# Order of the first two head pairs written out by hand, mask constants copied by ACT instead of DMA, bias loaded later, more output buffers

## Chip, cores, metric

The kernel runs on one core of a Trainium2 chip. The metric is device time in microseconds (us) of one execution. A ratio in this text is the mean time of one kernel's fast runs over the mean time of the other's fast runs of the same rounds; it is therefore not quite the ratio of the medians that are quoted. A profile is one execution, and its times count from the start of its span.

PE is TensorE's matmul part, PEld its weight loads, DVE is VectorE, ACT is ScalarE, POOL is GpSimd, and SP is SyncE, which only issues DMAs here. In the profile lines `qs` is q with its selection, `trm` and `tr` are transposes, `kTp` is k transposed, `kmm` and `km` are the extremes of k, `rq` the two signed parts of q, `ub` the bounds, `sc` scores, `e` exps, `acc` attention values, `mlp` a result of the MLP and `o` the output. An eviction is ACT's copy of a finished matmul result into a buffer.

## What the kernel computes

Four batches, eight heads, 768 positions, head size 64. Attention looks only at the six best chunks of 32 keys for each query; a gated MLP follows.

```python
k_min, k_max = min and max of k over each chunk of 32 keys
ub    = sum_d max(q*k_min, q*k_max)               # upper bound of a score for each query and chunk
ub    = where(causal by chunk, ub, -1e9)
mask  = (chunk of key is among the 6 largest ub) & (key <= query)
attn  = softmax(where(mask, q@k.T / sqrt(64), -1e9))
x     = (attn @ v) of all heads side by side       # (4, 768, 512)

h     = relu(x @ w_in);  u, v = halves of h
v_n   = (v - mean(v)) / sqrt(var(v) + 1e-6)
out   = (u * (w_spatial @ v_n + b_spatial[:, None])) @ w_out
```

## The kernel before: what the change touches

The work is cut into 16 pairs of heads, four per batch. Each pair has a preparation (k transpose, chunk extremes, q transpose, bounds, top six, selection, transposes and copies of the selection and q into an operand `a`) and then two times six groups of scores, each followed by an exp on ACT. One half of each key operand `kh` holds a mask constant, `expand`, which each buffer of the ring must be given once.

The program is written as a list of steps at "beats", and a scheduler sets the final order of instructions on each engine. Only for PE, and only for beats below zero, the written order is kept.

```python
NB = 4
kh_ring = [[ring.tile([P, S], F16, ...) for hi in range(2)] for i in range(NB)]

def init_kh(i):                       # the mask constant of ring place i
    for hi, (d0, d1) in enumerate(HALF):
        if i < 2:
            nc.scalar.copy(kh_ring[i][hi][d0:d1, :], expand)
        else:
            nc.sync.dma_start(out=kh_ring[i][hi][d0:d1, :], in_=expand)
# ... cut ...
def a_copy(self, hi):
    if self.i >= 8: return
    copy = nc.vector.tensor_copy if self.i == 0 and hi == 0 else nc.scalar.copy
    copy(self.a[:, :, hi, :], self.tr.rearrange("d (t s) -> d t s", s=P))
# ... cut: the output of one tile of 128 rows, six for each batch ...
o_sb = ml.tile([P, DM], F32, tag="o", name="o", bufs=3)
nc.scalar.copy(o_sb, o_ps)
nc.sync.dma_start(out=out[b, ti * P:(ti + 1) * P, :], in_=o_sb)
# ... cut: order of the start ...
at(B0, init_masks)                    # B0 = -30
at(B0, load_k, 0, 0, 1); at(B0, load_k, 0, 1, 1)
for i in range(NB):
    at(B0 if i < 2 else -8, init_kh, i)
for i, p in enumerate(pairs):
    t0 = i * BEATS                    # BEATS = 12
    if i == 1: t0 += 4
    if i == 0: ...                    # pair 0: one step after the other at B0 + 1
        continue
    at(t0 - 27, p.k_transpose); at(t0 - 22, p.k_max); at(t0 - 21, p.q_transpose)
    # ... cut ...
```

The softmax here doesn't subtract the row's maximum and nothing guards it: scores larger than these inputs give would overflow.

## Time and profile before

| | before |
|---|---|
| median of the runs | 211.34 us (211.15 to 211.51) |
| span of the profiled execution | 209.2 us |
| first exp (pair 0) | 16.70 us |
| pair 1's first exp | 25.46 us |
| first MLP eviction | 58.41 us |

The chain of waits of the kernel before, as shares of the span by engine:

```profile
PE 65%; ACT 17%; DVE 5%; POOL 5%; DMA 4%; issue 3%; POOLq 0%; ACTq 0%
```

The shares alone say "PE-bound". The table by stretches says where. Its columns are the stretch in us, its length, the busy time of PE, PEld, DVE, ACT and POOL with the number of instructions, the granted clock, and the DMA share and GB/s. (The DMA share is the time of all packets added up over the time of 16 engines; it can exceed 1.) Kernel before:

```profile
25.46:58.41 32.95, 29.08 (x446) 22.08 (x445) 28.81 (x92) 30.94 (x68) 26.86 (x35) 1.00 1.98 171
61.00:105.00 44.00, 43.32 (x499) 27.84 (x497) 40.38 (x118) 37.00 (x80) 17.68 (x18) 1.00 1.73 130
105.00:150.00 45.00, 44.53 (x450) 26.46 (x449) 38.54 (x123) 37.06 (x81) 8.34 (x9) 1.00 0.81 142
150.00:185.00 35.00, 34.77 (x268) 18.20 (x267) 18.05 (x39) 23.28 (x49) 4.33 (x5) 1.00 0.44 102
```

From 61 to 185 us PE hardly idles, so time won earlier should be kept there. From 25 to 58 us ACT is fullest, with PE and DVE close behind. Before that single waits set the time: from 9 to 16 us PE is busy 4.16 us of 7, DVE 2.73 and ACT 3.07. Only POOL, which issues the loads of q, k and v one after the other, is busy throughout. These are ACT's (start, duration, what; in brackets the idle time before it and what ended it), kernel before:

```profile
10.85 0.70 ACT L215 ACTIVATE rq<-trm 128x640 f16<-128x640 f16 x1 [0.93 <-DVE rq L213]
11.45 0.78 ACT L197 COPY kh_1_89<-kTp 64x768 f16<-64x768 f16 x1
14.99 0.80 ACT L260 COPY a<-trm 128x768 f16<-128x768 f16 x1 [2.76 <-PE trm L254]
16.70 1.57 ACT L274 ACTIVATE e<-sc 128x512 f16<-128x512 f32 x3 [0.90 <-PE sc L272]
...
18.80 2.78 ACT L274 ACTIVATE e<-sc 128x512 f16<-128x512 f32 x6
22.23 1.25 ACT L274 ACTIVATE e<-sc 128x512 f16<-128x512 f32 x3 [0.65 <-PE sc L269]
```

And these are the three places where PE stood for a DMA in the start, timeline of the kernel before:

```profile
9.60 0.69 PE L208 MATMUL trm<-identity,qs_83 128*128 128x128 f16 x5 [2.91 <-DMA qs_83<-in_q_dram]
...
18.66 0.50 PE L173 MATMUL kTp<-identity,k 128*128 128x128 f16 x6 [0.39 <-DMA k<-in_k_dram]
...
21.64 0.44 PE L208 MATMUL trm<-identity,qs_84 128*128 128x128 f16 x5 [0.65 <-DMA qs_84<-in_q_dram]
```

The first is pair 0's q. The other two are pair 2's k and q, whose transposes stand in PE's order among pair 0's scores, so that those scores wait for pair 2's landing.

The end, ACT's timeline of the kernel before, shows the third to the sixth of the last six output copies:

```profile
202.25 0.59 ACT L440 COPY o<-mlp 128x512 f32<-128x512 f32 x1 [0.28 <-PE mlp L391]
204.32 1.79 ACT L440 COPY o<-mlp 128x512 f32<-128x512 f32 x3 [1.48 <-DMA out_dram<-o]
```

The fourth copy waits 1.48 us until an earlier output DMA has freed one of three buffers.

### The profile page before, as it was taken

The numbers are of one execution on the slowest core, as the hardware profiler recorded it, in microseconds if no ns is written. First come the engines' busy times: TensorE is split into PE (matmuls) and PEld (weight loads), VectorE is DVE, ScalarE is ACT, GpSimd is POOL, SyncE is SP. The second block draws the span as 40 slices with busy tenths as digits, with TensorE's granted clock in tenths as the row PEclk, the third lists the DMA queues.
The fourth block names the chain that finished last, engine by engine and source line by source line (L and its number), as shares of the span: only waits on it lengthen the run. The fifth ranks groups of instructions, "written<-read, shape, count | busy, mean of one in ns | idle before, by whom it ended". The sixth has DMA issues, their size and how long they took to land.

```text
span 209.2 us, 5074 instructions
## 1 busy us (share of the span) xinstructions
PE 187.0 (89%) x1922; PEld 114.8 (55%) x1922; DVE 154.1 (74%) x453; ACT 155.7 (74%) x323; POOL 79.6 (38%) x99
## 2 busy tenths in 40 slices
PE   0359799798999999999999999999999999999991
PEld 0256577575666665656664656556555554444440
DVE  6348989888889989899888799888547356366520
ACT  4638798999997899785979996668999821666033
POOL 7995697595991364237114111111111110000000
PEclk9999999999999999999999999999999999999998
DMA  6999999999999699979998932948792115530365
GB/s 38 158 128 155 141 172 155 181 177 173 172 163 165 50 117 125 152 128 123 155 258 183 175 55 50 128 86 148 192 172 66 38 28 100 179 147 3 75 157 219
DMA packets 115496, 27.66 MB, mean 132 GB/s; under 512 B 110352, under 2 KB 111888, under 8 KB 115472
## 3 DMA queue, kind: packets, MB, share of 16 engines
q0 software_dynamic: 76512, 12.19, 88.2%
q1 hardware_dynamic: 38960, 15.15, 36.0%
q8 instruction: 15, 0.25, 0.5%
q14 instruction: 9, 0.07, 0.1%
HBM read 24.38 MB, written 6.29 MB: 147 GB/s over the span
## 4 chain that ended last, share of the span: by engine, by line
PE 65%; ACT 17%; DVE 5%; POOL 5%; DMA 4%; issue 3%; POOLq 0%; ACTq 0%
PE mlp L391 38%; PE sc L269 11%; ACT e L274 9%; PE acc L292 8%; ACT a L260 3%; DMA k<-in_k_dram 3%; PE ub L225 2%; POOL qs_83 L341 2%; PE kTp L173 2%; PE tr L208 1%; DVE vn L415 1%; POOL k L332 1%; ACT o L440 1%; DMA out_dram<-o 1%; ACT u L423 1%
## 5 line engine op out<-in xcount | busy, mean ns | idle before, releaser
L274 ACT ACTIVATE e<-sc 128x512 f16<-128x512 f32 x192 | 97.2, 552 | 15.6 <-PE sc L269 13.7
L391 PE MATMUL mlp<-w_in_sb,xT 128*128 128x512 f16 x192 | 52.9, 379 | 0.0
L281 POOL TENSOR_SCALAR_AFFINE_SELECT e<-e 128x768 f16<-128x768 f16 x24 | 20.8, 867 | 68.7 <-ACT e L274 68.6
L292 PEld LDWEIGHTS <-e 128*128 128x128 f16 x672 | 31.6, 97 | 17.5 <-DVE x_2178 L300 1.0
L391 PE MATMUL mlp<-vn,wsT 128*128 128x512 f16 x144 | 37.3, 379 | 0.0
L440 ACT COPY o<-mlp 128x512 f32<-128x512 f32 x24 | 14.1, 590 | 20.8 <-PE mlp L391 18.6
L403 DVE BATCH_NORM_STATS2 stats<-vraw 128x6 f32<-128x512 f32 x24 | 16.6, 693 | 13.5 <-ACT vraw L401 13.1
L391 PE MATMUL mlp<-w_out_sb,gT 128*128 128x512 f16 x96 | 25.1, 379 | 0.0
L391 PEld LDWEIGHTS <-xT 128*128 128x128 f16 x192 | 17.2, 97 | 12.4 <-issue 0.4
L430 DVE SCALAR_TENSOR_TENSOR g<-mlp,b_col,u 128x512 f16<-128x512 f32 x24 | 17.9, 747 | 7.3 <-PE mlp L391 6.2
L391 PEld LDWEIGHTS <-wsT 128*128 128x128 f16 x144 | 12.9, 98 | 10.4
L181 DVE TENSOR_REDUCE kmm<-kTp 128x24 f16<-128x768 f16 x16 | 15.1, 945 | 3.4 <-PE kTp L173 3.2
L401 ACT ACTIVATE vraw<-mlp 128x512 f32<-128x512 f32 x24 | 14.4, 601 | 3.0 <-PE mlp L391 3.0
L423 ACT ACTIVATE u<-mlp 128x512 f16<-128x512 f32 x24 | 14.3, 597 | 1.7 <-PE mlp L391 1.5
L330 POOL DMA_DIRECT2D k<-in_k_dram x14 | 14.4, 1042 | 2.5 <-PE kTp L173 1.8
L185 DVE TENSOR_REDUCE kmm<-kTp 128x24 f16<-128x768 f16 x16 | 15.1, 943 | 0.0
L173 PE MATMUL kTp<-identity,k 128*128 128x128 f16 x96 | 8.6, 230 | 6.3 <-POOL tri L144 5.9
L391 PEld LDWEIGHTS <-gT 128*128 128x128 f16 x96 | 9.1, 98 | 8.9
L292 PE MATMUL acc<-vt_80,e 128*128 128x65 f16 x252 | 13.7, 193 | 0.0
L415 DVE TENSOR_SCALAR vn<-vraw,mv,rstd 128x512 f16<-128x512 f32 x24 | 11.8, 544 | 2.2 <-ACT rstd L413 2.1
L292 PE MATMUL acc<-vt_81,e 128*128 128x65 f16 x252 | 13.0, 193 | 0.2 <-DVE x_3135 L300 0.2
L299 DVE RECIPROCAL rec<-acc 128x6 f32<-128x6 f32 x32 | 6.0, 187 | 6.5 <-PE acc L292 6.2
(165 smaller groups left out, 337.5 us busy)
## 6 DMA issues: line engine op xcount, KB each, us to landing
out_dram<-o SPq DMA_DIRECT2D x24, 256.0 KB, 2.3
k<-in_k_dram POOLq DMA_DIRECT2D x14, 192.0 KB, 8.2
vt_80<-in_v_dram POOLq DMA_DIRECT2D x3, 384.0 KB, 8.7
qs_84<-in_q_dram POOLq DMA_DIRECT2D x6, 192.0 KB, 7.5
vt_81<-in_v_dram POOLq DMA_DIRECT2D x3, 384.0 KB, 8.8
ws_raw<-in_moe_w_spatial_dram POOLq DMA_DIRECT2D x6, 192.0 KB, 7.6
w_in_sb<-in_moe_w_in_dram POOLq DMA_DIRECT2D x8, 128.0 KB, 6.6
qs_85<-in_q_dram POOLq DMA_DIRECT2D x4, 192.0 KB, 7.2
```

The lines of the kernel that those rows point to most:

```text
L181: nc.vector.tensor_reduce(self.kmm[:, 0, :], self.kT.rearrange("d (c ch) -> d c ch", ch=CHUNK), axis=AX.X, op=Alu.max)
L185: nc.vector.tensor_reduce(self.kmm[:, 1, :], self.kT.rearrange("d (c ch) -> d c ch", ch=CHUNK), axis=AX.X, op=Alu.min, negate=True)
L269: mm(sc[:, col:col + n], lhsT=self.kh[hi][:, t * P:(t + 1) * P], rhs=self.a[:, q0 // P:(q0 + n) // P, hi, :], start=True, stop=not diag)
L274: nc.scalar.activation(out=self.e[hi][:, g * 512:g * 512 + width], in_=sc[:, 0:width], func=Act.Exp, scale=scale)
L281: nc.gpsimd.affine_select(out=blk, in_=blk, compare_op=Alu.is_ge, fill=0.0, base=0, channel_multiplier=-1, pattern=[[0, NQT], [1, P]])
L292: mm(self.av[:, qi, :], lhsT=self.e[hi][:, c:c + P], rhs=self.v[hi][:, t, 0:D + 1], start=first and n == 0, stop=last and n == len(blocks) ...
L330: nc.gpsimd.dma_start(out=t[:, :, :, 1 - hi, :].rearrange("p x t d -> p (x t) d"), in_=source(k, b, h, 2))
L391: mm(st[group][:, 0:cols], lhsT=lhsT, rhs=rhs, start=(j == 0), stop=(j == n - 1))
L403: nc.vector.bn_stats(stats, st["vraw"][:, ti, :])
L423: nc.scalar.activation(st["u"][:, ti, :], h, func=Act.Relu)
L430: nc.vector.scalar_tensor_tensor(g, in0=vs, scalar=b_col[:, ti:ti + 1], in1=st["u"][:, ti, :], op0=Alu.add, op1=Alu.mult)
L440: nc.scalar.copy(o_sb, o_ps)
```

## The change

The intent is a shorter start. (1) The mask constants of ring places 2 and 3 are copied by ACT instead of by four SP DMAs. (2) The preparation of pairs 0 and 1 is one list in a hand-written order, PE's written order is kept up to beat 5, pair 1's first copy of `a` goes to DVE, and pairs 2 and 3 are prepared later. (3) The second half of the first k load, which is pair 1's k, is issued before the masks are made, and the spatial bias is loaded later, by POOL. (4) The output tile has six buffers. The diff is shortened; left out are `init_ring(2)`, `init_kh(0)` and `init_kh(1)`, which are now listed at the start by name, and two conditions rewritten without effect.

```diff
     def init_kh(i):
         for hi, (d0, d1) in enumerate(HALF):
-            if i < 2:
-                nc.scalar.copy(kh_ring[i][hi][d0:d1, :], expand)
-            else:
-                nc.sync.dma_start(out=kh_ring[i][hi][d0:d1, :], in_=expand)
+            nc.scalar.copy(kh_ring[i][hi][d0:d1, :], expand)
@@
-            copy = nc.vector.tensor_copy if self.i == 0 and hi == 0 else nc.scalar.copy
+            copy = nc.vector.tensor_copy if self.i < 2 and hi == 0 else nc.scalar.copy
@@
-        nc.sync.dma_start(out=b_col, in_=moe_b_spatial...)
+        nc.gpsimd.dma_start(out=b_col, in_=moe_b_spatial...)
@@
-                o_sb = ml.tile([P, DM], F32, tag="o", name="o", bufs=3)
+                o_sb = ml.tile([P, DM], F32, tag="o", name="o", bufs=6)
@@
-    at(B0, init_masks)
     at(B0, load_k, 0, 0, 1)
     at(B0, load_k, 0, 1, 1)
+    at(B0, init_masks)
@@
-        if i == 1:
-            t0 += 4
-        if i == 0:
-            ...                                  (the list of pair 0, cut)
+        if i < 2:
             continue
-        at(t0 - 27, p.k_transpose)
+        t0 += 4 if i < 4 else 0
+        at(t0 - (22 if i < 4 else 27), p.k_transpose)
@@
+    p, n = pairs[0:2]
+    for beat, *step in (
+            ... (B0 + 1, p.top, 1), (B0 + 1, p.select), (B0 + 1, init_kh, 2), (B0 + 1, init_kh, 3),
+            (B0 + 1, p.a_transpose, 0), (B0 + 1, p.a_copy, 0), (B0 + 1, n.k_transpose),
+            (B0 + 1, p.a_transpose, 1), (B0 + 1, n.k_max), (B0 + 1, p.a_copy, 1), (B0 + 1, n.k_min),
+            (B0 + 1, n.k_operand, 0), (0, n.q_transpose), (1, n.q_parts, 0), (1, n.k_bounds), (1, n.q_parts, 1),
+            (1, n.k_operand, 1), (2, n.bounds), (3, n.top, 0), (3, n.top, 1), (4, n.select), ...):
+        at(beat, *step)
@@
-        for beat in sorted(b for b in beats if b < 0):
+        for beat in sorted(b for b in beats if b < 6):
```

More of the change, by code (lines that the diff above doesn't have):

```diff
@@ L195, in k_operand @@
             d0, d1 = HALF[1 - hi]
-            copy = nc.scalar.copy if self.i == 0 else nc.vector.tensor_copy
+            copy = nc.scalar.copy if self.i < 1 else nc.vector.tensor_copy
             copy(self.kh[hi][d0:d1], self.kT[d0:d1])
@@ L213, in q_parts @@
                 nc.vector.tensor_scalar(self.rq[:, 0, P:S], in0=self.tr[:, P:S], scalar1=0.0, scalar2=None, op0=Alu.max)
-            elif self.i == 0:
+            elif self.i < 1:
                 nc.scalar.activation(self.rq[:, 1, P:S], self.tr[:, P:S], func=Act.Relu, scale=-1.0)
@@ L374, in load_b @@
     def load_b():
-        nc.sync.dma_start(out=b_col, in_=moe_b_spatial.rearrange("(to ti) -> ti to", ti=P))
+        nc.gpsimd.dma_start(out=b_col, in_=moe_b_spatial.rearrange("(to ti) -> ti to", ti=P))
     def mlp(b):
@@ L471 @@
     at(B0, init_ring, 1)
-    at(-6, init_ring, 2)
-    for i in range(NB):
-        at(B0 if i < 2 else -8, init_kh, i)
+    at(B0, init_ring, 2)
+    at(B0, init_kh, 0)
+    at(B0, init_kh, 1)
     at(40, load_b)
@@ L494 @@
         t0 = i * BEATS
-        if i == 1:
-            t0 += 4
-        if i == 0:
-            for step in ((p.k_transpose,), (p.k_max,), (p.k_min,), (p.k_operand, 0), (p.q_transpose,),
-                         (p.q_parts, 0), (p.k_bounds,), (p.q_parts, 1), (p.k_operand, 1), (p.bounds,), (p.top, 0), (p.top, 1), (p.select,),
-                         (p.a_transpose, 0), (p.a_copy, 0), (p.a_transpose, 1), (p.a_copy, 1)):
-                at(B0 + 1, *step)
+        if i < 2:
             continue
-        at(t0 - 27, p.k_transpose)
+        t0 += 4 if i < 4 else 0
+        at(t0 - (22 if i < 4 else 27), p.k_transpose)
         at(t0 - 22, p.k_max)
@@ L519 @@
         at(t0 - 6, p.a_copy, 1)
+    p, n = pairs[0:2]
+    for beat, *step in (
+            (B0 + 1, p.k_transpose), (B0 + 1, p.k_max), (B0 + 1, p.k_min), (B0 + 1, p.k_operand, 0),
+            (B0 + 1, p.q_transpose), (B0 + 1, p.q_parts, 0), (B0 + 1, p.k_bounds),
+            (B0 + 1, p.q_parts, 1), (B0 + 1, p.k_operand, 1), (B0 + 1, p.bounds), (B0 + 1, p.top, 0),
+            (B0 + 1, p.top, 1), (B0 + 1, p.select), (B0 + 1, init_kh, 2), (B0 + 1, init_kh, 3), (B0 + 1, p.a_transpose, 0), (B0 + 1, p.a_copy, 0),
+            (B0 + 1, n.k_transpose), (B0 + 1, p.a_transpose, 1), (B0 + 1, n.k_max), (B0 + 1, p.a_copy, 1), (B0 + 1, n.k_min),
+            (B0 + 1, n.k_operand, 0),
+            (0, n.q_transpose), (1, n.q_parts, 0), (1, n.k_bounds), (1, n.q_parts, 1),
+            (1, n.k_operand, 1), (2, n.bounds), (3, n.top, 0), (3, n.top, 1), (4, n.select), (5, n.a_transpose, 0),
+            (5, n.a_copy, 0), (6, n.a_transpose, 1), (6, n.a_copy, 1)):
+        at(beat, *step)
     for j in range(NDO):
```

## The prediction

> **What bounds the kernel now.** The chain of waits gives PE 65% and ACT 17% of the span. The table by stretches shows three stages. From 61 to 185 us PE is busy over 98%, so what reaches 61 us earlier should end earlier. From 25.46 to 58.41 us ACT is busy 30.94 of 32.95 us, PE 29.08. Before that is a start of single dependent steps: the timeline has the first exp at 16.70 us and pair 1's first at 25.46. The end (185 to 209) is paced by PE, then by output.
>
> **The start.** The timeline has pair 0's q transposes at 9.60 us, 2.9 us idle for q's landing; those loads took 3.9 and 4.9 us from issue, the first k loads 3.2 and 3.5. Between lie four SP copies of mask constants, at 5 to 9 us. The DMA records show q/k packets falling from about 700 per us to 425 to 570 while those run. The Trainium skill ("DMA: Bandwidth & Descriptors", Issuing engines are not separate DMA queues) says that DMAs of all issuers share 16 DMA engines; this trace agrees. Without the copies I estimate that q lands 1.2 us earlier. ACT's kh copy and km copies (done at 9.92) then come last, so the bounds finish only about 1.0 us earlier.
>
> The four constants become ACT copies of 0.83 us: 3.3 us, placed by the instruction order after the second kh copy (ends 12.23, estimated 11.4 after), ahead of pair 0's copy of a. ACT idled there 2.76 us, so they delay it about 0.4 us. Estimate: first exp at 15.6 instead of 16.70 (-1.1).
>
> **Pair 1.** The order puts pair 1's k transpose between pair 0's two a transposes, its q transpose after the first score, and no longer puts pair 2's q transposes (waiting 0.7 us for a landing) among pair 0's scores. Pair 1's first a copy goes to DVE, saving ACT 0.7 us. Bounds in front of later scores may idle ACT 0.8 us. Estimate: pair 1's first exp at 23.5 instead of 25.46, so -2.0 in all. Pairs 2 and 3 have ACT as limit, with unchanged work: the lead stays near 2.0 at the first MLP eviction (58.41 before). PE's order from there is nearly the same, loads land before use, so it should reach the end.
>
> **The end.** The fourth of the last output copies waited 1.48 us for one of three o buffers (timeline, until 204.32). With six it does not; the last copy would end about 0.7 us earlier, bounded by PE's last group. I count -0.6.
>
> **Sum.** -2.0 - 0.6 = -2.6 us: 208.7 us; range 206.9 to 210.4. Faster by over 2% (under 207.1): 0.13; within 2%: 0.85; slower: 0.02.
>
> **Right or wrong.** Right if: pair 0's q transposes start before 8.6 us; first exp at 15.3 to 16.0; pair 1's first exp at 23 to 24; first MLP eviction at 56 to 57; no output copy waits for a DMA; PE over 98% busy in the middle. Wrong at its step if q's landing does not move, if ACT's constants delay the first exp past 16.2, if pair 1's first exp comes after 24.5, or if the first MLP eviction has not moved although pair 1 has.
>
> **What would make it wrong.** Upwards: pairs 2 and 3 take the lead back; DVE (28.81 of 32.95 us) and PE are nearly as full as ACT and their chains are now issued later. Downwards: ACT's 3.2 us of idle time between 16.70 and 58.41 shrinks too, up to about -5 in all. I expect no effect of b_col's later load.

## The result, and the profile after

The changed kernel took 208.62 us (median of four runs, 208.56 to 208.74), the kernel before 211.43 us in the same rounds (211.15 to 211.91). The ratio is 0.9866, with a 95% interval of 0.9847 to 0.9885. It is 2.8 us faster. The predicted time was 208.7 us.

The spans of the two profiles are 209.2 and 206.9 us, only 2.3 us apart. The profiled execution of the kernel before took 210.93 us, less than nearly all of its timed executions (210.72 to 212.28 in all rounds). So differences between the profiles understate the gain by about half a us, and where a size matters the timed runs are used.

The lead, that is how much earlier a mark comes in the changed kernel's profile than in that of the kernel before:

| mark | before | after | lead |
|---|---|---|---|
| pair 0's q transposes start | 9.60 | 8.45 | 1.15 |
| first exp | 16.70 | 15.29 | 1.41 |
| pair 1's first exp | 25.46 | 23.41 | 2.05 |
| pair 3's first exp | 41.30 | 39.81 | 1.49 |
| pair 4's first exp | 49.16 | 47.12 | 2.04 |
| pair 5's first exp | 55.94 | 54.66 | 1.28 |
| first MLP eviction | 58.41 | 57.10 | 1.31 |
| pair 9's first exp | 98.60 | 97.19 | 1.41 |
| pair 10's first exp | 109.01 | 107.07 | 1.94 |
| first of the last six output copies | 200.52 | 198.73 | 1.79 |
| span | 209.2 | 206.9 | 2.3 |

ACT's timeline of the changed kernel, the answer to the lines shown of before:

```profile
9.81 0.70 ACT L212 ACTIVATE rq<-trm 128x640 f16<-128x640 f16 x1
10.41 0.78 ACT L194 COPY kh<-kTp 64x768 f16<-64x768 f16 x1
11.09 3.36 ACT L150 COPY kh<-expand 64x768 f16<-64x768 f16 x4
14.60 0.80 ACT L257 COPY a<-trm 128x768 f16<-128x768 f16 x1
15.29 0.60 ACT L271 ACTIVATE e<-sc 128x512 f16<-128x512 f32 x1
16.20 1.13 ACT L271 ACTIVATE e<-sc 128x512 f16<-128x512 f32 x2 [0.30 <-PE sc L269]
...
18.61 3.21 ACT L271 ACTIVATE e<-sc 128x512 f16<-128x512 f32 x7 [0.77 <-PE sc L266]
```

The four constants take 3.36 us and end at 14.45, just as the transposes for the copy of `a` are done. They fill the hole that ACT had there (2.76 us in the kernel before) and delay nothing.

PE's timeline of the changed kernel: pair 0's q comes 1.15 us earlier. The other two waits for landings are gone: apart from this one and pair 0's first k (5.75 us), PE waits for no DMA up to 26 us.

```profile
8.45 0.69 PE L205 MATMUL trm<-identity,qs 128*128 128x128 f16 x5 [1.91 <-DMA qs<-in_q_dram]
```

What stands beside q's load is to be seen in the DMA view of the stretch from 5 to 9 us (queue, packets, MB, share of 16 engines). First the kernel before:

```profile
q0 software_dynamic: 2016, 0.25, 99.9%
q1 hardware_dynamic: 319, 0.39, 33.9%
```

The same view of the changed kernel:

```profile
q0 software_dynamic: 3159, 0.40, 155.5%
```

Queue q0 carries q and k here; q1 carries SP's four copies (and 63 packets of 4 bytes). Without those, q0 moves 3159 packets in place of 2016 in the same 4 us. Not all of that is due to the copies, as the changed kernel also asks for pair 1's k earlier; the clean comparison, with the same order of loads, is the experiment with the constants by DMA again. The Trainium skill ("DMA: Bandwidth & Descriptors", Issuing engines are not separate DMA queues) says that DMAs from all issuers end up on the same 16 engines; these views, and the clean comparison, agree.

The stages of the changed kernel, same columns as before:

```profile
25.46:58.41 32.95, 29.75 (x444) 22.12 (x441) 29.29 (x96) 30.34 (x66) 26.30 (x33) 1.00 1.97 171
61.00:105.00 44.00, 43.38 (x497) 27.88 (x496) 40.35 (x126) 36.68 (x78) 17.45 (x18) 1.00 1.79 141
105.00:150.00 45.00, 45.00 (x460) 26.70 (x459) 38.08 (x114) 37.95 (x83) 9.21 (x10) 1.00 0.85 136
150.00:185.00 35.00, 34.62 (x254) 17.94 (x253) 18.13 (x40) 22.63 (x48) 3.45 (x4) 1.00 0.42 104
```

PE is full from 61 us on, as before. The chain of waits of the changed kernel no longer has POOL in it, and has less of DMAs:

```profile
PE 69%; ACT 17%; DVE 8%; issue 2%; DMA 2%; POOL 0%; DVEq 0%; ACTq 0%; POOLq 0%
```

The end, ACT's timeline of the changed kernel:

```profile
201.32 0.58 ACT L437 COPY o<-mlp 128x512 f32<-128x512 f32 x1 [0.28 <-PE mlp L388]
202.19 0.58 ACT L437 COPY o<-mlp 128x512 f32<-128x512 f32 x1 [0.28 <-DMA out_dram<-o]
203.05 0.58 ACT L437 COPY o<-mlp 128x512 f32<-128x512 f32 x1 [0.28 <-PE mlp L388]
```

Each copy now follows PE's output group by 0.28 us; the one line that names a DMA has the same gap as its neighbours, so it is no wait of its own.

Two things in the table of leads were not in the prediction. The lead falls from 2.0 to 1.3 us between pairs 4 and 5. And it rises by 0.5 us near 107 us, long after the start. The timelines of ACT show what lies at the second place. Kernel before:

```profile
108.36 0.59 ACT L440 COPY o<-mlp 128x512 f32<-128x512 f32 x1 [0.48 <-DMA out_dram<-o]
```

Changed kernel:

```profile
106.36 0.58 ACT L437 COPY o<-mlp 128x512 f32<-128x512 f32 x1
```

It is the same wait for an output buffer as at the end, here in the first batch's outputs. Six outputs in a burst are not the reason here. The first of the three buffers was filled by 100.20 us, but SP issued its DMA only at 104.35, because SP first issued the transposing load of pair 10's `a`, which took it 3.55 us. SP's timeline of the kernel before:

```profile
100.71 3.55 SPq L249 DMA_TRANSPOSE a<-qs_85  x1
104.35 1.01 SPq L441 DMA_DIRECT2D out_dram<-o  x2
```

That output landed 3.9 us after its issue, and the waiting copy could start. ACT does its work in order in this trace: the exp whose scores PE had finished by 107.73 us starts at 108.84, behind the copy, though ACT stood idle for 0.48 us. PE feels it later: with three buffers in the changed kernel (next section) it waits 0.36 us at 112.19 us for DVE, and with six it does not.

### The profile page after: what moved, and what is told of

Same layout as the page of the kernel before. It is cut to its first block, busy times and chain, and to the rows that moved or that the text cites. A ratio compares the mean times of both kernels' runs of the same rounds, so it can differ in the third digit from the quotient of the medians.

```text
span 206.9 us, 5068 instructions
## 1 busy us (share of the span) xinstructions
PE 187.8 (91%) x1922; PEld 115.1 (56%) x1922; DVE 154.5 (75%) x454; ACT 158.1 (76%) x326; POOL 80.5 (39%) x100
## 4 chain that ended last, share of the span: by engine, by line
PE 69%; ACT 17%; DVE 8%; issue 2%; DMA 2%; POOL 0%; DVEq 0%; ACTq 0%; POOLq 0%
PE mlp L388 40%; PE sc L266 12%; ACT e L271 10%; PE acc L289 7%; PE kTp L170 2%; ACT a L257 2%; DVE kmm L178 2%; PE ub L222 2%; DMA k<-in_k_dram 2%; PE trm L251 2%; ACT vraw L398 1%; PE tr L205 1%; DVE vn L412 1%; DVE kmm L182 1%; ACT u L420 1%
## 5 line engine op out<-in xcount | busy, mean ns | idle before, releaser
L266 PE MATMUL sc<-a,kh 128*128 128x512 f16 (+3 forms) x256 | 65.5, 308 | 2.1 <-ACT e L271 1.5
L289 PE MATMUL acc<-vt,e 128*128 128x65 f16 x672 | 35.3, 193 | 0.7 <-DVE x L297 0.4
L266 PEld LDWEIGHTS <-kh 128*128 128x128 f16 x256 | 22.7, 98 | 13.3 <-issue 0.8
L232 DVE MAX8 max<-ub 128x8 f32<-128x8 f32 (+4 forms) x160 | 15.6, 165 | 5.1 <-PE ub L222 4.9
L178 DVE TENSOR_REDUCE kmm<-kTp 128x24 f16<-128x768 f16 x16 | 15.2, 948 | 3.7 <-PE kTp L170 2.7
L297 DVE TENSOR_TENSOR x<-acc,rec 128x384 f16<-128x384 f32 x32 | 17.6, 551 | 0.4
L336 POOL DMA_DIRECT2D qs<-in_q_dram x14 | 14.6, 1049 | 5.9 <-PE sc L266 5.9
L194 DVE COPY kh<-kTp 64x768 f16<-64x768 f16 x30 | 16.5, 549 | 0.5
```

Of the source, the lines that this page charges most:

```text
L178: nc.vector.tensor_reduce(self.kmm[:, 0, :], self.kT.rearrange("d (c ch) -> d c ch", ch=CHUNK), axis=AX.X, op=Alu.max)
L194: copy(self.kh[hi][d0:d1], self.kT[d0:d1])
L266: mm(sc[:, col:col + n], lhsT=self.kh[hi][:, t * P:(t + 1) * P], rhs=self.a[:, q0 // P:(q0 + n) // P, hi, :], start=True, stop=not diag)
L289: mm(self.av[:, qi, :], lhsT=self.e[hi][:, c:c + P], rhs=self.v[hi][:, t, 0:D + 1], start=first and n == 0, stop=last and n == len(blocks) ...
L297: nc.vector.tensor_tensor(self.x16[:, :, hi, :], in0=self.av[:, :, 0:D], in1=rec.to_broadcast([P, NQT, D]), op=Alu.mult)
```

## The experiments

Twelve kernels ran, all with five rounds against the kernel before. All were correct.

### Three output buffers again, in the changed kernel

```diff
-                o_sb = ml.tile([P, DM], F32, tag="o", name="o", bufs=6)
+                o_sb = ml.tile([P, DM], F32, tag="o", name="o", bufs=3)
```

> The changed kernel with three o buffers again instead of six. Theory A (read from the two traces: the lead over the kernel before grows from 1.4 to 1.95 us at the first batch's output copies near 109 us, and from 1.8 to 2.5 us at the last ones): the buffers are worth about 1.2 us in two places, so this run ends 1.0 to 1.3 us later than the changed kernel, its lead stays near 1.4 us from 58 to 195 us, and one output copy near 107 us and one near the end wait for an output DMA. Theory B (the prediction): the buffers count only in the last output group, so 0.6 us later, and the lead rises near 109 us all the same.

Measured: 209.66 us median, ratio 0.9922 (0.9892 to 0.9952), against 0.9866 of the changed kernel; its span is 207.95 us, against 206.90. The difference is 1.2 us by the ratios and 1.05 us by the spans. The lead is 1.41 us at pair 9 and 1.53 at pair 10 (1.94 with six buffers), so 0.41 us of the 1.05 is won near 107 us and the rest at the end. At the end the wait is back, ACT's timeline of this run:

```profile
202.74 1.82 ACT L437 COPY o<-mlp 128x512 f32<-128x512 f32 x3 [1.44 <-DMA out_dram<-o]
```

Theory A holds: the buffers count in two places, and for about twice what the prediction gave them. What it gave the end alone, 0.6, was about right.

### Six output buffers alone, in the kernel before

```diff
-                o_sb = ml.tile([P, DM], F32, tag="o", name="o", bufs=3)
+                o_sb = ml.tile([P, DM], F32, tag="o", name="o", bufs=6)
```

> The kernel before with six o buffers and nothing else. Theory A: 1.0 to 1.3 us faster than the kernel before, in two steps (about 0.5 us near 109 us, 0.7 us at the end), with nothing moved before 100 us. Theory B: 0.6 us faster, all of it in the last 10 us.

Measured: 210.17 us median, ratio 0.9930 (0.9909 to 0.9952), that is 1.5 us. One line gives half of the whole gain. The size in time is over theory A's, but the place is not as it said: in the profile the first step near 107 us is only 0.05 us, and the last 10 us give 0.7. ACT no longer waits near 107 us, but PE waits there for something else (list of waits of this run from 98 to 112 us: engine, line, what for, us in total, times, longest):

```profile
PEld L269 <- DMA a<-qs: 0.8, 1, 0.8
...
PE sc L269 <- DMA a<-qs: 0.3, 1, 0.3
```

This is the landing of pair 10's operand `a`, whose transposing load stands in SP's queue before the output DMAs. SP took 4.01 us to issue it in this profile (3.55 in the kernel before, 3.35 in the changed kernel), and it landed 7.7 us after the start of its issue (7.1 in both of those). In this profile the first wait, taken away, turned into the next one. That second wait comes and goes: in the profiles PE's matmuls wait 0.2 us or more for `a` here only where SP's issue took 4.0 us or more, and two variants of the changed kernel that are told below (the bias at the start, k transposes later) have it too. Why the issue takes longer in some of them was not looked into. The timed runs gain more than the one profile shows (1.5 us against 0.7 by the spans); the quick profiled execution of the kernel before, 0.8 us under the median of these rounds, makes up about all of that.

### The constants by DMA again, in the changed kernel

```diff
-            nc.scalar.copy(kh_ring[i][hi][d0:d1, :], expand)
+            if i < 2:
+                nc.scalar.copy(kh_ring[i][hi][d0:d1, :], expand)
+            else:
+                nc.sync.dma_start(out=kh_ring[i][hi][d0:d1, :], in_=expand)
```

> The changed kernel with the four mask constants of pairs 2 and 3 copied by SP DMA again; order and buffers stay changed. Theory A (the copies slow q's landing): pair 0's q transposes start at 9.4 to 9.7 us instead of 8.45, the first exp comes at 16.0 to 16.5 us instead of 15.29, and the run ends 0.4 to 1.0 us later. Rival: the q landing gained from the other order of loads; then q transposes stay near 8.5 us and the run is within 0.2 us of the changed kernel, or faster, as ACT is rid of 3.3 us of copies.

Measured: 209.94 us median, ratio 0.9920 (0.9903 to 0.9938), 1.1 us slower than the changed kernel. PE's timeline of this run:

```profile
10.11 0.69 PE L208 MATMUL trm<-identity,qs 128*128 128x128 f16 x5 [3.74 <-DMA qs<-in_q_dram]
```

Theory A holds, with more than it expected: q's transposes start at 10.11 us, later than in the kernel before (9.60), and the first exp at 16.84. The DMA view of this run from 5 to 9 us:

```profile
q0 software_dynamic: 2234, 0.28, 111.0%
q1 hardware_dynamic: 279, 0.35, 33.3%
```

Against the changed kernel, which has the same order of loads and 3159 packets on q0, this is what the copies alone take. The rival, that the new order of loads brought q earlier, fails: beside the SP copies the new order comes with a q that is 0.51 us later.

### The constants by ACT alone, in the kernel before

```diff
-            if i < 2:
-                nc.scalar.copy(kh_ring[i][hi][d0:d1, :], expand)
-            else:
-                nc.sync.dma_start(out=kh_ring[i][hi][d0:d1, :], in_=expand)
+            nc.scalar.copy(kh_ring[i][hi][d0:d1, :], expand)
@@
-    for i in range(NB):
-        at(B0 if i < 2 else -8, init_kh, i)
+    for i in range(2):
+        at(B0, init_kh, i)
@@
-                         ... (p.select,), (p.a_transpose, 0), ...
+                         ... (p.select,), (init_kh, 2), (init_kh, 3), (p.a_transpose, 0), ...
```

> The kernel before with only the four constants on ACT, after pair 0's second kh copy, as in the changed kernel; order of loads, pair order and three o buffers as before. Theory A: q transposes at 8.4 to 8.7 us instead of 9.60, first exp at 15.3 to 15.9 instead of 16.70, but in this order PE still stands before pair 2's q transposes and k transposes for landings, so pair 1's first exp gains less than the first exp did (24.6 to 25.2 instead of 25.46), and the run ends 0.2 to 0.8 us earlier than the kernel before. Rival: the constants are the whole gain of the start; then pair 1's first exp comes at 24.0 or sooner and the run ends 1.2 us or more earlier.

Measured: 211.32 us median, ratio 0.9995 (0.9974 to 1.0015): no gain. Yet q's transposes start at 7.94 us, earlier than theory A expected, and the first exp comes at 15.80 us, 0.90 earlier. At pair 1's first exp, 25.41 us, 0.05 is left, less than theory A's 0.3. PE's timeline of this run says where it went:

```profile
18.61 0.49 PE L170 MATMUL kTp<-identity,k 128*128 128x128 f16 x6 [1.16 <-DMA k<-in_k_dram]
...
21.52 0.44 PE L205 MATMUL trm<-identity,qs 128*128 128x128 f16 x5 [0.59 <-DMA qs<-in_q_dram]
```

Pair 2's k landed at the same time as before (18.61, before 18.66), as POOL issues the loads back to back in both kernels, and in the old order its transposes stand ahead of pair 0's remaining scores. PE came there earlier and waited 1.16 us in place of 0.39. The Trainium skill ("PSUM — Partial Sum Buffer", Engine vs sequencer instructions) says that matmuls start and finish in program order; this trace agrees, as pair 0's scores, with all their data there, start after the landing. Both theories expected some gain at the end, so both were too high.

### The new order alone

The changed kernel with two of the edits above: constants by SP DMA and three output buffers.

```diff
-            nc.scalar.copy(kh_ring[i][hi][d0:d1, :], expand)
+            if i < 2:
+                nc.scalar.copy(kh_ring[i][hi][d0:d1, :], expand)
+            else:
+                nc.sync.dma_start(out=kh_ring[i][hi][d0:d1, :], in_=expand)
@@
-                o_sb = ml.tile([P, DM], F32, tag="o", name="o", bufs=6)
+                o_sb = ml.tile([P, DM], F32, tag="o", name="o", bufs=3)
```

> The changed kernel's order, with the constants by SP DMA and three o buffers as before. From the last runs: the constants alone changed nothing (ratio 0.9995), and order plus six buffers gave 0.992 where six buffers alone gave 0.993. Theory (order and constants need each other: each alone only moves the wait to the next landing or the next step): this run is within 0.5 us of the kernel before, ratio 0.997 to 1.001, with the first exp near 16.8 us and the lead over the kernel before at 58 us under 0.4 us. Rival (each part is worth its share by itself): ratio 0.993 to 0.995, that is 1.0 to 1.5 us faster.

Measured: 211.20 us median, ratio 0.9996 (0.9969 to 1.0022). Pair 1's first exp is 0.70 us earlier than before, but q's transposes start at 10.15 us and at the first MLP eviction (58.43) nothing is left. The theory holds: by itself the order is worth nothing either, as far as intervals of about 0.25% on each side can tell. Together the runs are:

| constants by ACT | new order | six buffers | ratio to before |
|---|---|---|---|
| yes | no | no | 0.9995 |
| no | yes | no | 0.9996 |
| no | no | yes | 0.9930 |
| yes | yes | no | 0.9922 |
| no | yes | yes | 0.9920 |
| yes | yes | yes | 0.9866, again 0.9871 |

The buffers give 0.5 to 0.8% in every pairing (0.9996 to 0.9920 is the largest step, 0.9922 to 0.9871 the smallest). Constants and order give 0.6 to 0.8% together and nothing apart. (Constants with buffers in the old order were not run, and the parts of the order, that is PE's written order, the first copy of `a` on DVE, pairs 2 and 3 later and the order of loads, were not taken apart.)

The traces say what the order costs. From pair 2's first exp to pair 5's the three profiles with the old order (before, six buffers alone, constants alone) take 22.7 us, and the profiles with the new order 23.4 us: the changed kernel and its repeat, three buffers, constants by DMA, the order alone. This holds whether the lead at pair 2 is 0.45 or 2.0 us. So the order alone wins 0.70 us up to pair 1 and pays 0.7 back; with the constants on ACT it wins 2.0 and pays the same 0.7.

### Pair 3's preparation at its old place

```diff
-        t0 += 4 if i < 4 else 0
-        at(t0 - (22 if i < 4 else 27), p.k_transpose)
+        t0 += 4 if i < 3 else 0
+        at(t0 - (22 if i < 3 else 27), p.k_transpose)
```

> The changed kernel with pair 3's preparation at its old place (four beats earlier; pair 2 stays shifted). In the changed kernel the lead over the kernel before falls from 2.0 us at pair 2 to 1.5 us at pair 3 and 1.3 us at pair 5. Theory A (the later place of pair 3's chain costs it: ACT waits for pair 3's a transposes): pair 3's first exp at 39.2 to 39.5 us instead of 39.81, the lead stays at 1.8 us or more at the first MLP eviction (56.6 or sooner instead of 57.10), and the run is 0.3 to 0.7 us faster than the changed kernel. Theory B (VectorE is full there, 8.92 of 9 us busy from 34 to 43 us, whatever the order): first MLP eviction within 0.2 us of 57.10 and the run within 0.3 us of the changed kernel, or slower.

Measured: 209.51 us median, ratio 0.9909 (0.9890 to 0.9929), about 0.9 us slower than the changed kernel. Pair 3's first exp is at 39.72 us, 0.09 earlier, but pair 2's is at 31.91, later than the 31.25 of the changed kernel, and the first MLP eviction at 57.54. Theory A fails: the later place of pair 3 is not what costs the lead. Of theory B the time agrees ("or slower"), which is no proof of its reason.

### Pair 1's small bounds copies on DVE

```diff
-                copy = nc.gpsimd.tensor_copy if 2 <= self.i < 4 else nc.scalar.copy
+                copy = nc.vector.tensor_copy if self.i == 1 else nc.gpsimd.tensor_copy if 2 <= self.i < 4 else nc.scalar.copy
```

> The changed kernel with pair 1's two small bounds copies (64x48) on VectorE, right after its rq, instead of on ACT behind three exps. In the changed kernel pair 1's bounds matmuls wait for them until 17.89 us and ACT then stands 0.77 us before the fourth exp. Theory A (this wait is on the chain of the start): the fourth exp comes 0.5 to 0.9 us earlier (17.7 to 18.1 us instead of 18.61), pair 1's first exp at 22.5 to 23.0 instead of 23.41, and 0.2 to 0.7 us of it reaches the end. Theory B (pair 1's landing or the later pairs give the pace): pair 1's first exp earlier, but the first MLP eviction within 0.15 us of 57.10, and no gain.

Measured: 208.83 us median, ratio 0.9871 (0.9851 to 0.9892), no difference to the changed kernel. A miss on the way: the fourth exp comes later, at 19.05 us, and so do pair 1's first exp (23.86) and the first MLP eviction (57.46). Neither theory expected that; of both only B's "no gain" came true. The timeline of this run:

```profile
17.07 0.69 DVE L189 COPY km<-kmm 64x48 f16<-64x48 f16 x2
...
17.80 0.49 DVE L214 TENSOR_SCALAR rq<-trm 128x640 f16<-128x640 f16 x1
...
19.05 0.60 ACT L271 ACTIVATE e<-sc 128x512 f16<-128x512 f32 x1 [1.87 <-PE sc L266]
```

The two copies took 0.69 us on DVE (0.48 on ACT) and stand in front of the second half of rq, for which the bounds also wait. ACT's idle time grew from 0.77 to 1.87 us in the place of the copies that left.

### The bias loaded at the start again

```diff
-        nc.gpsimd.dma_start(out=b_col, in_=moe_b_spatial...)
+        nc.sync.dma_start(out=b_col, in_=moe_b_spatial...)
```

> The changed kernel with the spatial bias loaded by SP at the start again. Its 768 packets of 4 bytes run before the first k packets. All theories: the first k transpose moves by no more than 0.2 us and the run is within 0.3 us of the changed kernel, so the later load is no part of the gain; a rival that it delays k and everything after it would show 0.5 us or more.

Measured: 209.01 us median, ratio 0.9870 (0.9850 to 0.9891), as expected, and the first k transpose starts at 5.73 us (5.75 in the changed kernel). The later bias is no part of the gain that these runs could show. The profile of this run has the wait for pair 10's `a` (0.36 us of PE at 107.08; SP's issue took 4.21 us), so that its lead does not rise at pair 10: 1.45 us, against 1.94.

### Pair 1's bounds two beats later

```diff
-            (1, n.k_operand, 1), (2, n.bounds), (3, n.top, 0), (3, n.top, 1), (4, n.select), ...
+            (1, n.k_operand, 1), (4, n.bounds), (4, n.top, 0), (4, n.top, 1), (4, n.select), ...
```

> The changed kernel with pair 1's bounds matmuls two beats later (after pair 0's fourth and fifth score instead of before them). In the changed kernel those matmuls wait for ACT's bounds copies until 17.89 us, the scores stand behind them in PE's order, and ACT idles 0.77 us before the fourth exp. Expected: the fourth exp follows at 17.8 to 18.0 us instead of 18.61. Theory A (that wait is on the chain): pair 1's first exp 0.3 to 0.8 us earlier than 23.41 and 0.2 us or more of it kept at the end. Theory B (VectorE's chain for pair 1, with the selection ending at 21.25, sets the pace): pair 1's first exp within 0.3 us of 23.41 and the run within 0.3 us of the changed kernel.

Measured: 208.65 us median (208.46 to 208.69), ratio 0.9859 (0.9835 to 0.9882); the changed kernel on the same chip, in the run told last, 208.89 (208.61 to 209.15) and 0.9871. The fourth exp comes at 17.79 us without a wait, as expected. Pair 1's first exp is at 23.23, which is 0.18 before the first profile of the changed kernel and 0.33 before its repeat. Theory B holds for the most part: what ACT won there it mostly lost again before pair 1's first exp, as the transposes of pair 1's selection start at 21.32 us, in the changed kernel at 21.30. The run is at best 0.24 us faster by the medians; the intervals overlap, so a gain is not shown.

### The k transposes of pairs 4 to 6 later too

```diff
-        at(t0 - (22 if i < 4 else 27), p.k_transpose)
+        at(t0 - (22 if i < 7 else 27), p.k_transpose)
```

This one aims at the lead lost between pairs 4 and 5. PE's timeline of the changed kernel at that place, with ACT's next exp:

```profile
52.42 0.22 PE L266 MATMUL sc<-a,kh 128*128 128x128 f16 x1 [0.67 <-ACT e L271]
52.47 0.50 PE L310 MATMUL trm<-identity,x 128*128 128x128 f16 x6
52.80 0.29 PE L289 MATMUL acc<-vt,e 128*128 128x65 f16 x4
53.11 0.44 PE L205 MATMUL tr<-identity,qs 128*128 128x128 f16 x5
53.38 0.50 PE L289 MATMUL acc<-vt,e 128*128 128x65 f16 x11
53.72 0.50 PE L170 MATMUL kTp<-identity,k 128*128 128x128 f16 x6
54.05 0.35 PE L289 MATMUL acc<-vt,e 128*128 128x65 f16 x6
...
54.66 0.60 ACT L271 ACTIVATE e<-sc 128x512 f16<-128x512 f32 x1 [0.44 <-PE sc L266]
```

After the last score of pair 4, which waits 0.67 us, 38 small matmuls follow in a row (the 32 in the expectation leave out the six of the second line), and ACT runs dry.

> The changed kernel with the k transposes of pairs 4 to 6 five beats later as well. In the changed kernel the lead is still 2.0 us at pair 4's first exp and 1.3 us at pair 5's: PE there has all six scores of pair 4's second head first, waits 0.67 us for ACT to free a score buffer with the last one, and then does 32 small matmuls in a row, so that ACT idles 0.44 us; the kernel before has that last score after them. This variant's order has it after them again. Theory A (the small loss of lead is that order): no 0.67 us wait of PE for ACT near 52 us, pair 5's first exp at 54.1 us or sooner instead of 54.66, first MLP eviction at 56.3 to 56.7 instead of 57.10, and a run 0.3 to 0.7 us faster. Theory B (engines are full there and the lead is lost in any order): first MLP eviction within 0.2 us of 57.10, or later, and no gain.

Measured: 209.73 us median, ratio 0.9903 (0.9875 to 0.9931), 0.7 us slower than the repeat of the changed kernel (0.9871). The local part of theory A came true in part: the 0.67 us wait is gone, and the first MLP eviction is at 56.74 us, a lead of 1.67. But pair 5's first exp is at 54.91, later than the 54.66 of the changed kernel, and at pair 8 the lead is down to 0.92. Theory A is not confirmed as a whole: without this order at 52 us the MLP starts earlier, but the lead falls below that of the changed kernel (1.42 at pair 8) further on. More than that is lost in this profile by the wait for pair 10's `a`: PE waits 0.92 us at 108.17 us, SP's issue took 4.71 us, and the lead falls from 0.91 at pair 9 to 0.35 at pair 10, where that of the changed kernel rises. The six timed runs lie in two groups, 208.94 to 209.35 and 210.10 to 210.21, as they would if only some executions had this wait; that was not shown.

### Both last edits at once

```diff
-            (1, n.k_operand, 1), (2, n.bounds), (3, n.top, 0), (3, n.top, 1), (4, n.select), ...
+            (1, n.k_operand, 1), (4, n.bounds), (4, n.top, 0), (4, n.top, 1), (4, n.select), ...
@@
-        at(t0 - (22 if i < 4 else 27), p.k_transpose)
+        at(t0 - (22 if i < 7 else 27), p.k_transpose)
```

> Both edits at once: pair 1's bounds two beats later, and the k transposes of pairs 4 to 6 five beats later. If both theories A hold, the gains add to 0.5 to 1.2 us against the changed kernel; if both theories B hold, it is within 0.3 us of it. If only one gains, this run shows whether the other takes it back.

Measured: 209.41 us median, ratio 0.9904 (0.9878 to 0.9930). As the edit before it alone: the later k transposes take back whatever the later bounds may give.

### The changed kernel again

No edit.

> The changed kernel itself again, beside the other three on one chip, so that differences of a few tenths are read against it. Expected ratio to the kernel before 0.985 to 0.988, first exp at 15.2 to 15.5 us, pair 1's first exp at 23.3 to 23.9, first MLP eviction at 57.0 to 57.5.

Measured: 208.89 us median, ratio 0.9871 (0.9847 to 0.9896), first exp 15.38, pair 1's first exp 23.56, first MLP eviction 57.24. The result repeats.

## Why the prediction was right, and where only its sum was

The total was right: 208.7 us predicted, 208.62 measured. Point by point:

- **Earlier q.** "Without the copies I estimate that q lands 1.2 us earlier." The q transposes start 1.15 us earlier, and with the copies back they start at 10.11 us. The cause is right, and shown by experiment. That the number fits so well is luck: by single profiles the copies are worth 1.66 us in either order of loads (9.60 against 7.94, 10.11 against 8.45), the new order of loads takes 0.51 back, and in the nine profiles without copies and with the new order q starts anywhere from 7.88 to 8.71 us. The bounds do not follow each of these tenths: with q at 7.88 (three buffers again) the first exp is at 15.29 as with 8.45, because, as the prediction said, ACT's copies for the bounds then come last (PE's bounds wait 0.49 us for them at 9.84 in the changed kernel).
- **The constants fit ACT's hole.** "They delay it about 0.4 us" was too careful: they delay nothing, and the first exp came at 15.29 us, where 15.6 was predicted. Of its 1.41 us the constants alone give 0.90; the rest comes with the order, which puts pair 0's first score before pair 1's q transposes.
- **Pair 1's first exp.** 23.5 us predicted, 23.41 measured. Right. What the prediction did not see is that its two parts are no sum: it gave 1.1 us to the constants and 0.9 to the order, as if each stood by itself. Apart, they are worth nothing (0.9995 and 0.9996). With the constants alone PE runs into the landing of pair 2's k. With the order alone pair 0's q still lands late, and the 0.70 us gained by pair 1 are gone at 58 us.
- **"The lead stays near 2.0 at the first MLP eviction"** is the step that failed: it was 1.31 us there and 1.41 from then to pair 9. It rests on "Pairs 2 and 3 have ACT as limit, with unchanged work" and on PE's order being nearly the same from there. ACT's work was nearly unchanged, but it waited more: from pair 1's first exp to the first MLP eviction it is busy 31.11 of 33.69 us, before 30.94 of 32.95. The new order itself takes 0.7 us longer from pair 2 to pair 5, with any lead (see "The new order alone"). That "their chains are now issued later" stood among its reasons to be wrong, and fits this; which of the later steps costs the time is not shown.
- **"I count -0.6" for the output buffers** is the mis-sized term: they are worth 1.2 us in the changed kernel and 1.5 us in the kernel before (the intervals do not tell these two apart). The prediction had read only the 1.48 us wait of the last batch. The 0.48 us wait of the first batch's outputs stands in the same profile, in a stage where PE is over 98% busy; with three buffers put back into the changed kernel, 0.41 us is lost there, because the exps stood behind the waiting copy on ACT.
- **PE stays full from 61 to 185 us, and the lead is carried to the end.** Right: 43.38 of 44, 45.00 of 45 and 34.62 of 35 us busy. No effect of the later bias: right (0.9870 with the old place). Of the conditions in "Right if" two are missed by a hair: the first exp (15.29 us) and the first MLP eviction (57.10 us).

The lead overestimated at 58 us (2.0 in place of 1.3 to 1.4) and the buffers underestimated (0.6 in place of 1.2) are of like size and opposite sign. The sum was nearer to the truth than its terms.

What stays open: why the new order takes 0.7 us longer between pairs 2 and 5, which shows as a fall of the lead between pairs 4 and 5. It is seen in the trace together with PE's wait of 0.67 us; three other orders (pair 3 earlier, k transposes later, both last edits) were all slower in total. No version here clearly beats the changed kernel.

## What to carry to other kernels

When the start of a kernel is a chain of single waits, taking one wait away may be worth nothing until the next one in the engine's order is moved too; so test the parts of such a change both alone and together, and read the mark after the next, not only the first. Look for every place where the same buffer runs out, not only the longest wait: a short wait of an engine that works in order can hold up a full engine behind it. The Trainium skill ("Perfetto Trace Analysis", Optimization Strategy) names too few buffers as a possible cause of repeated gaps; here one wait in each of two output groups, not a repeated gap, was half of the gain. A right total can hide two wrong terms.

## What the Trainium skill lacked or had wrong

- "DMA: Bandwidth & Descriptors", Issuing engines are not separate DMA queues: right that queues share the engines, but with no size for what one queue takes from another. Here 279 packets (0.35 MB) of SP's queue in 4 us stood beside 2234 packets of the loads' queue, which moved 3159 without them in the same order of loads, and the transposes that wait for a load on the chain began 1.66 us later (10.11 against 8.45 us).
- "Trainium Kernel Development and Optimization", Best Practices, advises double buffers. Here three output buffers cost 1.2 to 1.5 us of 211, in two ways: at the end a burst of tiles, 0.87 us apart, is made faster than its DMAs free the buffers (a wait of 1.48 us), and near 107 us SP issued the first output's DMA only 4.15 us after its copy had ended, behind a transposing load (a wait of 0.48 us). Six buffers removed both.
- "Perfetto Trace Analysis", Optimization Strategy, says to find what blocks a gap and make it start sooner. It doesn't warn that the gap may only move: 0.90 us won at the first exp were 0.05 us one pair later, and the 0.77 us gap of ACT became 1.87 us when a copy was moved to DVE.
